# Batch 0 of an attention and GEGLU kernel in three parts of queries, with its first q and k loaded uncast

## The chip, the cores and the metric

The kernel runs on one core of a Trainium2 chip. The metric is the device time of one execution in microseconds (us), lower is better. The names of the engines in the profile are PE (TensorE), PEld (its weight loads), ACT (ScalarE), DVE (VectorE), POOL (GpSimd) and SP (the queue of SyncE). "The opening" is the time up to the first FFN block that is computed on all its 512 tokens with nothing of batch 0's attention left to do.

## The reference, cut to what matters

Sliding-window attention with a linear bias, on 8 batches, 8 heads, 576 tokens and head size 64, then an FFN on the 4608 tokens together.

```python
scores = scale * np.matmul(q, k.transpose(0, 1, 3, 2))
mask = (rel >= 0) & (rel < window)               # window = 128
scores = np.where(mask, scores + bias[None], -1000000000.0)
...                                              # softmax over the keys
x = attn_out.transpose(0, 2, 1, 3).reshape(B * S, H * D)
g = x @ w_gate                                   # 512 -> 1536
gelu = 0.5 * g * (1.0 + erf(g * inv_sqrt2))
return (gelu * (x @ w_val)) @ w_out              # 1536 -> 512
```

The kernel takes and gives float32 and computes in bf16.

## The kernel before

Everything after batch 0 is a dense stream of matmuls, with the attention of later batches laid between FFN blocks. Only batch 0 has nothing in front of it to hide behind. It is done in two parts of queries, 320 and 256. One part goes through these steps: transposes of q and k on PE and copies out of PSUM; scores on PE; exponentials on ACT; a multiplication by the mask on DVE; row sums on PE; a reciprocal on DVE; a spread of the reciprocals over partitions on PE with copies out; values on PE; a multiplication on DVE, which writes `xT`, the input of the FFN.

```python
# loads of batch 0: all on POOL, which casts float32 to bf16 on the way
load_runs(0, 0, 4)                  # q and k, heads 0 to 3, tokens 0 to 383
...
nc.gpsimd.affine_select(out=ident, ...)
load_runs(0, 4, 8)                  # heads 4 to 7
nc.gpsimd.iota(tmpl, ...)           # template of the mask
...                                 # two selects on tmpl
load_runs(1, 0, 8)                  # tokens 384 to 575
...
load_v(0)
for n in range(4):
    load_w(step * n, step * (n + 1))        # gate and value weights, by quarters
...
# the opening, in PE's program order (keep_busy(n): n matmuls of zeros before the next bank)
keep_busy(9)
first((0, 1))                       # transposes of heads 0 to 3
keep_busy(2)
scores(0, 0, (0, 1), ...)
...
spread_pe(0, 0)
values(0, 0, range(4))              # xT of 320 tokens
sums(0, 1)
for f in range(2):
    gate_val(0, f, 0, 320)          # FFN blocks 0 and 1, first 320 tokens
spread_pe(0, 1)
gate_val(0, 2, 0, 320)
values(0, 1, range(4))              # xT of the other 256 tokens
for f in range(3):
    gate_val(0, f, 320, 512)
# then blocks 3 to 11 on 512 tokens each
```

The matmuls of zeros are there to bring PE up to its full rate and to keep it there while it waits. Exponentials of the template (`emask`, eight on ACT) give the mask for all heads.

The softmax here doesn't subtract the row's maximum and nothing guards it: scores larger than these inputs give would overflow.

## Time and profile before

| | kernel before |
|---|---|
| time, median of 4 runs | 366.65 us (366.53 to 366.88) |
| span of the profiled run | 364.9 us |
| PE, DVE, ACT, POOL busy | 96%, 52%, 51%, 30% |
| first transposes of q / first scores | 5.15 / 7.58 us |
| first FFN matmul | 22.02 us |
| block 3 (first on 512 tokens) / block 6 | 30.59 / 35.77 us |

The busy shares say that PE is the bound on the whole; the times of the opening say where it isn't. Columns of the timeline: start us, length us, engine, line, operation, output<-inputs, shapes, count; in brackets the idle time before it and what ended it.

```profile
5.88 0.60 PE L70 MATMUL ps<-zeros 128*128 128x512 bf16 x2
6.57 0.36 PEld L139 LDWEIGHTS <-ks 128*64 128x64 bf16 x12 [0.58 <-DMA ks<-in_k_dram]
```

A pair of warm-up matmuls takes 0.60 us here, so PE is at its full rate by 5.88 us. The nine warm-up matmuls before that took 4.02 us, one every 0.43 us; a pair at that pace takes 1.03 us, as later traces show. This is called the half rate below. The first weights of k are loaded at 6.57 us, released by k's landing; it is the last load that the first scores need.

### The profile page before, as it was taken

The page shows a single profiled execution, that of the slowest core. Times are in us where ns is not written, and L with a number is a line of the kernel's source. Part 1 is how long each engine was busy: PE and PEld are TensorE (multiplying, and loading weights), DVE is VectorE, ACT ScalarE, POOL GpSimd, SP SyncE. Part 2 cuts the span into 40 slices and gives each one's busy share as a digit, 9 for nine tenths or more (in the row PEclk, how much of TensorE's full clock was granted, in tenths as well). Part 3 has the DMA queues.
Part 4 walks back from the last instruction along what each step waited for, and adds up shares of the span by engine and source line. Part 5 has one row for each costly group of instructions (what it writes and reads, how often), then busy time and mean ns, then how long its engine had stood idle before and what let it go on. Part 6 is the DMA issues. An engine that isn't in the chain of part 4 may idle for free.

```text
span 364.9 us, 6652 instructions
## 1 busy us (share of the span) xinstructions
PE 351.6 (96%) x2638; PEld 170.7 (47%) x2682; DVE 189.0 (52%) x307; ACT 187.2 (51%) x339; POOL 108.1 (30%) x140
## 2 busy tenths in 40 slices
PE   8889999999999999999999999999999999999995
PEld 3455545444454445444444444444444444444442
DVE  4794448533795469474547554745564404302320
ACT  5953487435966376933783278436842223323321
POOL 8945859923519203900940040000000000000000
PEclk9999999999999999999999999999999999999999
DMA  9999999999999994999991992092206030011002
GB/s 105 133 202 180 171 160 183 178 152 194 140 150 98 147 105 81 147 106 224 116 202 53 224 91 89 32 216 58 88 31 131 0 115 2 0 60 58 0 31 86
DMA packets 151168, 41.41 MB, mean 113 GB/s; under 512 B 138816, under 2 KB 144448, under 8 KB 151136
## 3 DMA queue, kind: packets, MB, share of 16 engines
q0 software_dynamic: 112608, 18.88, 67.9%
q1 hardware_dynamic: 38528, 22.10, 28.4%
q8 instruction: 21, 0.34, 0.4%
q14 instruction: 11, 0.09, 0.1%
HBM read 42.47 MB, written 9.51 MB: 142 GB/s over the span
## 4 chain that ended last, share of the span: by engine, by line
PE 86%; ACT 8%; DVE 2%; issue 1%; POOL 1%; POOLq 0%; ACTq 0%; DVEq 0%
PE ps L292 50%; PE ps L308 23%; ACT P L181 6%; PE ps L273 4%; PE ps L174 4%; PE ps L232 2%; PE ps L255 1%; DVE xT L279 1%; DVE P L184 1%; ACT L181 1%; ACT emask L359 1%; PE ps L153 1%; DVE r L241 0%; POOL ks L115 0%; ACT osb L313 0%
## 5 line engine op out<-in xcount | busy, mean ns | idle before, releaser
L297 DVE TENSOR_TENSOR hT<-ps,gelu 128x512 bf16<-128x512 f32 (+2 forms) x111 | 74.4, 674 | 121.8 <-PE ps L292 107.1
L296 ACT ACTIVATE gelu<-ps 128x512 bf16<-128x512 f32 (+2 forms) x111 | 64.9, 586 | 120.0 <-PE ps L292 119.8
L292 PE MATMUL ps<-xT,wg 128*128 128x512 bf16 (+2 forms) x430 | 111.0, 373 | 1.7 <-DVE xT L279 0.7
L292 PE MATMUL ps<-xT,wv 128*128 128x512 bf16 (+2 forms) x435 | 110.4, 373 | 0.6
L308 PE MATMUL ps<-wo,hT 128*128 128x512 bf16 x413 | 97.2, 380 | 1.5 <-issue 0.8
L181 ACT ACTIVATE P<-ps 128x512 bf16<-128x512 f32 x144 | 74.3, 629 | 6.9 <-PE ps L174 6.8
L292 PEld LDWEIGHTS <-wv 128*128 128x128 bf16 x444 | 43.3, 98 | 50.5 <-issue 0.5
L292 PEld LDWEIGHTS <-wg 128*128 128x128 bf16 x444 | 41.9, 98 | 49.8 <-issue 2.3
L184 DVE TENSOR_TENSOR P<-P,emask 128x1024 bf16<-128x1024 bf16 x72 | 48.3, 685 | 31.2 <-ACT P L181 30.9
L308 PEld LDWEIGHTS <-hT 128*128 128x128 bf16 x432 | 39.7, 98 | 49.0 <-issue 4.4
L95 POOL DMA_DIRECT2D vb<-in_v_dram x40 | 33.7, 867 | 71.1 <-PE ps L273 70.4
L313 ACT COPY osb<-ps 128x512 f32<-128x512 f32 x36 | 21.7, 602 | 37.2 <-PE ps L308 32.8
L95 POOL DMA_DIRECT2D qs<-in_q_dram x35 | 29.7, 878 | 25.5 <-DMA qT<-qs 12.9
L95 POOL DMA_DIRECT2D ks<-in_k_dram x35 | 29.6, 882 | 9.6 <-DMA qs<-in_q_dram 6.6
L241 DVE RECIPROCAL r<-ps 128x320 f32<-128x320 f32 (+1 forms) x16 | 30.7, 1938 | 2.6 <-PE ps L232 2.6
L174 PE MATMUL ps<-qT,kT 64*128 64x256 bf16 (+1 forms) x384 | 23.5, 245 | 2.2 <-ACT kT L147 0.6
L279 DVE TENSOR_TENSOR xT<-ps,rb 128x320 bf16<-128x320 f32 (+1 forms) x64 | 24.7, 448 | 0.5 <-DMA rb<-rd 0.5
L174 PEld LDWEIGHTS <-kT 64*128 64x128 bf16 x384 | 12.9, 94 | 17.2 <-issue 12.7
L273 PE MATMUL ps<-P,vb 128*64 128x128 bf16 (+2 forms) x384 | 18.4, 243 | 0.1
L273 PEld LDWEIGHTS <-vb 128*64 128x64 bf16 x384 | 14.7, 110 | 6.8 <-issue 6.8
L232 PE MATMUL ps<-P,ones 128*32 128x128 bf16 (+2 forms) x384 | 10.8, 243 | 1.3 <-DVE P L184 1.1
L232 PEld LDWEIGHTS <-ones 128*32 128x32 bf16 x384 | 7.9, 96 | 5.5 <-issue 4.7
(50 smaller groups left out, 98.7 us busy)
## 6 DMA issues: line engine op xcount, KB each, us to landing
out_dram<-osb SPq DMA_DIRECT2D x36, 256.0 KB, 2.3
rb<-rd SPq DMA_DIRECT2D x8, 576.0 KB, 7.4
vb<-in_v_dram POOLq DMA_DIRECT2D x32, 128.0 KB, 5.7
qs<-in_q_dram POOLq DMA_DIRECT2D x28, 128.0 KB, 6.9
ks<-in_k_dram POOLq DMA_DIRECT2D x28, 128.0 KB, 6.3
wg<-in_moe_w_gate_dram POOLq DMA_DIRECT2D x4, 384.0 KB, 10.7
wv<-in_moe_w_val_dram POOLq DMA_DIRECT2D x4, 384.0 KB, 11.9
wo<-in_moe_w_out_dram POOLq DMA_DIRECT2D x2, 768.0 KB, 11.3
```

The costliest lines, as they stand in the source:

```text
L95: nc.gpsimd.dma_start(out=t[lo:128, j, :].rearrange("p (h d) -> p h d", h=H), in_=src[b][:, 128 * j - 64 + lo:128 * j + 64, :].rearrange(" ...
L174: nc.tensor.matmul(out=ps[:, col:col + 128 * n].rearrange("p (n t) -> p n t", n=n), lhsT=blocks(kT, b, i, c, j, 1).rearrange("p n t -> p ( ...
L181: nc.scalar.activation(out=dst, in_=src, func=AF.Exp, scale=0.125)
L184: nc.vector.tensor_tensor(out=dst, in0=dst, in1=m, op=ALU.mult)
L232: nc.tensor.matmul(out=ps[32 * c:32 * c + 32, a:e], lhsT=ones[:, min(j, 1), i, :], rhs=prob(b, s, c, i, j, e - a), start=(i == 0 and j == ...
L241: nc.vector.reciprocal(sumrow[b][:, lo:hi], ps[:, 0:hi - lo])
L273: nc.tensor.matmul(out=ps[64 * i:64 * i + 64, a:e], lhsT=vb[b % 2][:, j, 64 * h:64 * h + 64], rhs=prob(b, s, c, i, j, e - a), start=(j == ...
L279: nc.vector.tensor_tensor(out=xT[:, c, b * S + lo:b * S + hi], in0=ps[:, 0:hi - lo], in1=recip[b][:, c, lo:hi], op=ALU.mult)
L292: nc.tensor.matmul(out=ps[:, 0:hi - lo], lhsT=w[:, c, 128 * f:128 * (f + 1)], rhs=xT[:, c, t0 + lo:t0 + hi], start=(c == 0), stop=(c == 3))
L296: nc.scalar.activation(out=gl[:, 0:hi - lo], in_=pg[:, 0:hi - lo], func=AF.Gelu)
L297: nc.vector.tensor_tensor(out=hid[g][:, f, lo:hi], in0=pv[:, 0:hi - lo], in1=gl[:, 0:hi - lo], op=ALU.mult)
L308: nc.tensor.matmul(out=po, lhsT=hid[g][:, f, 128 * t:128 * (t + 1)], rhs=wo[:, f, :], start=(f == 0), stop=(f == NF - 1))
```

## The change

Its intent: q and k of the first queries should arrive sooner, because they come on the SP and ACT queues beside POOL's own loads; a smaller first part (192 tokens) should be through attention sooner; and six FFN blocks instead of three should be begun before the last part of the attention is done (the first three of them on those 192 tokens), so that PE has useful work meanwhile. The loads on SP and ACT come uncast, so DVE casts. The core of the diff:

```diff
-PART = ((0, 320), (320, 576))
+PART = ((0, 320), (320, 576), (0, 192), (192, 320))
...
-    load_runs(0, 0, 4)
+    raw = h_pool.tile([128, NF, 512], BF16, name="hT")...bitcast(FP32)
+    load_run(0, raw[0], q, nc.sync)          # tokens 0 to 191, uncast
+    load_run(0, raw[1], k, nc.scalar)
...
+    load_run(1, runs(qs[0], 1), q, nc.gpsimd)    # tokens 192 to 575, cast by POOL
     nc.gpsimd.affine_select(out=ident, ...)
-    load_runs(0, 4, 8)
     ...                                          # template of the mask
+    load_run(1, runs(ks[0], 1), k, nc.gpsimd)
+    load_v(0, (0, 1))
+    load_w(0, step)
...
-    keep_busy(9)
-    first((0, 1))
...
+    for w in (0, 1):
+        dve(out=runs((qs, ks)[w][0], 0), in_=raw[w])
+    keep_busy(7)
+    for w in (0, 1):
+        transpose_runs(0, w, range(4), dve)
+        keep_busy(2)
+    scores_first()
...
+    scores2(0, (1, 2), lambda: (spread_pe(0, 2, (dve, dve)), values(0, 2, range(4))))
+    scores(0, 1, (0, 1), lambda: (keep_busy(3), sums(0, 3)))
...
+    gate_val(0, 0, 0, 192, tails)
+    gate_val(0, 1, 0, 192, tails)
+    values(0, 3, range(4))
...
+    for f in range(3):
+        gate_val(0, f, 192, 320)
+    gate_val(0, 3, 0, 320)
     spread_pe(0, 1)
-    gate_val(0, 2, 0, 320)
+    gate_val(0, 4, 0, 320)
     values(0, 1, range(4))
-    for f in range(3):
+    gate_val(0, 5, 0, 320)
+    for f in range(6):
         gate_val(0, f, 320, 512)
```

More of the change, by code (lines that the diff above doesn't have):

```diff
@@ L12 @@
 ENG = mybir.EngineType
-PART = ((0, 320), (320, 576))
+PART = ((0, 320), (320, 576), (0, 192), (192, 320))
 PIECES = (((0, 0, 192), (1, 64, 320), (2, 192, 320)),
-          ((2, 0, 128), (3, 0, 256), (4, 128, 256)))
-PCOL = ({0: 64, 1: 256}, {4: 0, 2: 128, 3: 256})
+          ((2, 0, 128), (3, 0, 256), (4, 128, 256)),
+          ((0, 0, 192), (1, 64, 192)),
+          ((1, 0, 128), (2, 0, 128)))
+PCOL = ({0: 64, 1: 256}, {4: 0, 2: 128, 3: 256}, {0: 0, 1: 192})
 @with_exitstack
@@ L101, in load_qk, with load_run, load_v @@
         load(ks[b % 2], k, b)
-    RUNS = ((0, 128, 3), (384, 96, 2))
+    RUNS = ((0, 96, 2), (192, 128, 3))
     def runs(t, n):
         first, parts, r = RUNS[n]
-        lo = 1536 * n
+        lo = 1024 * n
         return t.rearrange("p j x -> p (j x)")[0:parts, lo:lo + 512 * r].rearrange(
             "p (h x) -> p h x", h=H)
-    def load_runs(n, h0, h1):
+    def load_run(n, dst, src, engine):
         first, parts, r = RUNS[n]
-        for t, src in ((qs[0], q), (ks[0], k)):
-            nc.gpsimd.dma_start(
-                out=runs(t, n)[:, h0:h1, :],
-                in_=src[0][h0:h1, first:first + parts * r, :].rearrange(
-                    "h (p r) d -> p h (r d)", r=r))
-    def load_v(b):
-        load(vb[b % 2], v, b)
+        engine.dma_start(
+            out=dst,
+            in_=src[0][:, first:first + parts * r, :].rearrange("h (p r) d -> p h (r d)", r=r))
+    def load_v(b, js=range(5)):
+        load(vb[b % 2], v, b, js)
     def load_w(lo, hi):
@@ L131, in by_pair, with transpose_runs @@
         return t.rearrange("p j c t -> p (j c t)").rearrange("p (c x) -> p c x", c=4)
-    def transpose_runs(n, what, c, ps):
+    def transpose_runs(n, what, cs, copy):
         first, parts, r = RUNS[n]
         src = runs((qs, ks)[what][0], n)
-        for x in range(r):
-            for i in (0, 1):
-                nc.tensor.transpose(
-                    out=ps[64 * i:64 * i + 64, parts * x:parts * x + parts],
-                    in_=src[:, 2 * c + i, 64 * x:64 * x + 64],
-                    identity=ident[0:parts, 0:parts])
-    def untangle(copy, n, what, c, ps):
-        first, parts, r = RUNS[n]
-        dst = by_pair((qT, kT)[what][0])[:, c, 64 + first:64 + first + parts * r]
-        copy(out=dst.rearrange("p (x r) -> p x r", r=r),
-             in_=ps[:, 0:parts * r].rearrange("p (r x) -> p x r", r=r))
+        ps = bank().bitcast(BF16)
+        for k, c in enumerate(cs):
+            for x in range(r):
+                lo = parts * (r * k + x)
+                for i in (0, 1):
+                    nc.tensor.transpose(
+                        out=ps[64 * i:64 * i + 64, lo:lo + parts],
+                        in_=src[:, 2 * c + i, 64 * x:64 * x + 64],
+                        identity=ident[0:parts, 0:parts])
+        for k in range(0, len(cs), 2):
+            lo = parts * r * k
+            dst = by_pair((qT, kT)[what][0])[
+                :, cs[k]:cs[k] + 2, 64 + first:64 + first + parts * r]
+            copy(out=dst.rearrange("p c (x r) -> p c x r", r=r),
+                 in_=ps[:, lo:lo + 2 * parts * r].rearrange("p (c r x) -> p c x r", c=2, r=r))
     def transpose(b, what, c, copy):
@@ L184, in mask, with scores2, scores_first, scores @@
         nc.vector.tensor_tensor(out=dst, in0=dst, in1=m, op=ALU.mult)
-    def scores2(b):
-        P = p2_pool.tile([128, 4, 2, 128], BF16, name="P2")
-        probs2[b] = P
-        ps = [bank(), bank()]
-        for c in range(4):
-            for i in (0, 1):
-                score(b, c, i, 2, 2, 1, ps[i], 128 * c)
-        for i in (0, 1):
-            exp(P[:, :, i, :], ps[i].rearrange("p (c n) -> p c n", c=4))
-        mask(P.rearrange("p c i n -> p (c i) n"), emask[:, :, 0:128])
-    def scores(b, s, cs, then=None):
+    def scores2(b, js=(2,), then=None):
+        pss = []
+        for j in js:
+            ps = [bank(), bank()]
+            pss.append(ps)
+            for c in range(4):
+                for i in (0, 1):
+                    score(b, c, i, j, 2, 1, ps[i], 128 * c)
+        if then:
+            then()
+        for j, ps in zip(js, pss):
+            P = p2_pool.tile([128, 4, 2, 128], BF16, name="P2")
+            probs2[b, j] = P
+            for i in (0, 1):
+                exp(P[:, :, i, :], ps[i].rearrange("p (c n) -> p c n", c=4))
+            lo = 128 * (2 - j)
+            mask(P.rearrange("p c i n -> p (c i) n"), emask[:, :, lo:lo + 128])
+    def scores_first():
+        pss = []
+        for c in range(4):
+            ps = [bank(), bank()]
+            pss.append(ps)
+            for j, a, e in PIECES[2]:
+                for i in (0, 1):
+                    col = PCOL[2][j]
+                    nc.tensor.matmul(
+                        out=ps[i][:, col:col + e - a],
+                        lhsT=by_pair(kT[0])[64 * i:64 * i + 64, c, 128 * j:128 * j + 128],
+                        rhs=by_pair(qT[0])[64 * i:64 * i + 64, c, 64 + a:64 + e],
+                        start=True, stop=True)
+        for c, ps in enumerate(pss):
+            P = p_pool[0].tile([128, 2, 512], BF16, name="P")
+            probs[0, 2, c] = P
+            for i in (0, 1):
+                exp(P[:, i, 0:320], ps[i][:, 0:320])
+            mask(P[:, :, 0:192], emask[:, 2 * c:2 * c + 2, 64:256])
+            mask(P[:, :, 192:320], emask[:, 2 * c:2 * c + 2, 0:128])
+    def scores(b, s, cs, then=None, later=None):
         pss = []
@@ L215, in scores, with prob @@
                 exp(P[:, i, :], ps[i])
-            mask(P.rearrange("p i (n x) -> p i n x", n=2),
-                 emask[:, 2 * c:2 * c + 2, :].unsqueeze(2).to_broadcast((128, 2, 2, 256)))
-    def prob(b, s, c, i, j, n):
-        if (s, j) == (0, 2):
-            return probs2[b][:, c, i, 0:n]
-        return probs[b, s, c][:, i, PCOL[s][j]:PCOL[s][j] + n]
+            args = (P.rearrange("p i (n x) -> p i n x", n=2),
+                    emask[:, 2 * c:2 * c + 2, :].unsqueeze(2).to_broadcast((128, 2, 2, 256)))
+            if later is None:
+                mask(*args)
+            else:
+                later.append(args)
+    def prob(b, s, c, i, j, a, e):
+        if s == 3 or (s, j) == (0, 2):
+            return probs2[b, j][:, c, i, 0:e - a]
+        return probs[b, s, c][:, i, PCOL[s][j]:PCOL[s][j] + e - a]
     sumrow, recip = {}, {}
@@ L228, in sums @@
         ps = bank()
-        for j, a, e in PIECES[s]:
+        for n, (j, a, e) in enumerate(PIECES[s]):
             for i in (0, 1):
@@ L233, in sums @@
                         out=ps[32 * c:32 * c + 32, a:e],
-                        lhsT=ones[:, min(j, 1), i, :], rhs=prob(b, s, c, i, j, e - a),
-                        start=(i == 0 and j == 2 * s), stop=(i == 1 and j == 2 * s + 2),
+                        lhsT=ones[:, min(j, 1), i, :], rhs=prob(b, s, c, i, j, a, e),
+                        start=(i == 0 and n == 0), stop=(i == 1 and n == len(PIECES[s]) - 1),
                         skip_group_check=True)
-        if s == 0:
+        if b not in sumrow:
             sumrow[b] = r_pool.tile([128, S], FP32, name="r")
@@ L249, in spread_dma, with spread_pe @@
                 in_=d[:, i, :].unsqueeze(0).to_broadcast((64, 4, S)))
-    def spread_pe(b, s):
+    def spread_pe(b, s, copies=(nc.scalar.copy, nc.vector.tensor_copy)):
         lo, hi = PART[s]
@@ L260, in spread_pe @@
         for c, ps in enumerate(pss):
-            copy = nc.scalar.copy if c % 2 == 0 else nc.vector.tensor_copy
-            copy(out=recip[b][:, c, lo:hi], in_=ps[:, 0:hi - lo])
+            copies[c % 2](out=recip[b][:, c, lo:hi], in_=ps[:, 0:hi - lo])
     def values(b, s, cs):
@@ L269, in values @@
             pss.append(ps)
-            for j, a, e in PIECES[s]:
+            for n, (j, a, e) in enumerate(PIECES[s]):
                 for i in (0, 1):
@@ L275, in values @@
                         lhsT=vb[b % 2][:, j, 64 * h:64 * h + 64],
-                        rhs=prob(b, s, c, i, j, e - a),
-                        start=(j == 2 * s), stop=(j == 2 * s + 2), skip_group_check=True)
+                        rhs=prob(b, s, c, i, j, a, e),
+                        start=(n == 0), stop=(n == len(PIECES[s]) - 1),
+                        skip_group_check=True)
         for c, ps in zip(cs, pss):
@@ L283, with gate_val @@
     hid = {}
-    def gate_val(g, f, lo=0, hi=512):
+    def gate_val(g, f, lo=0, hi=512, later=None):
         if g not in hid:
@@ L294, in gate_val, with act @@
                     rhs=xT[:, c, t0 + lo:t0 + hi], start=(c == 0), stop=(c == 3))
-        gl = g_pool.tile([128, 512], BF16, name="gelu")
-        nc.scalar.activation(out=gl[:, 0:hi - lo], in_=pg[:, 0:hi - lo], func=AF.Gelu)
-        nc.vector.tensor_tensor(out=hid[g][:, f, lo:hi], in0=pv[:, 0:hi - lo],
-                                in1=gl[:, 0:hi - lo], op=ALU.mult)
+        def act():
+            gl = g_pool.tile([128, 512], BF16, name="gelu")
+            nc.scalar.activation(out=gl[:, 0:hi - lo], in_=pg[:, 0:hi - lo], func=AF.Gelu)
+            nc.vector.tensor_tensor(out=hid[g][:, f, lo:hi], in0=pv[:, 0:hi - lo],
+                                    in1=gl[:, 0:hi - lo], op=ALU.mult)
+        if later is None:
+            act()
+        else:
+            later.append(act)
     acc = {}
@@ L315, in out_half @@
             nc.sync.dma_start(out=out[r0:r0 + 128, :], in_=osb)
-    load_runs(0, 0, 4)
+    raw = h_pool.tile([128, NF, 512], BF16, name="hT").rearrange(
+        "p f t -> p (f t)").bitcast(FP32)
+    raw = [raw[0:96, 1024 * w:1024 * w + 1024].rearrange("p (h x) -> p h x", h=H)
+           for w in (0, 1)]
+    load_run(0, raw[0], q, nc.sync)
+    load_run(0, raw[1], k, nc.scalar)
     zeros = consts.tile([128, 512], BF16, name="zeros")
@@ L336 @@
             base=base, pattern=[[step, 128]], channel_multiplier=chan)
-    load_runs(1, 0, 8)
+    load_run(1, runs(ks[0], 1), k, nc.gpsimd)
+    load_v(0, (0, 1))
+    step = DFF // 4
+    load_w(0, step)
     for c in range(4):
@@ L341 @@
             base=-32 * c, pattern=[[-16, 2], [0, 64]], channel_multiplier=1)
-    load_v(0)
-    step = DFF // 4
-    for n in range(4):
+    load_w(step, 2 * step)
+    load_v(0, (2, 3, 4))
+    for n in (2, 3):
         load_w(step * n, step * (n + 1))
@@ L363 @@
     act, dve = nc.scalar.copy, nc.vector.tensor_copy
-    def first(cs):
-        for w in (0, 1):
-            if w and len(cs) == 2:
-                keep_busy(2)
-            for c in cs:
-                ps = bank().bitcast(BF16)
-                transpose_runs(0, w, c, ps)
-                untangle(act if c == 3 else dve, 0, w, c, ps)
-    def rest(cs, copy):
-        for c in cs:
-            for w in (0, 1):
-                ps = bank().bitcast(BF16)
-                transpose_runs(1, w, c, ps)
-                untangle(copy, 1, w, c, ps)
-    keep_busy(9)
-    first((0, 1))
-    keep_busy(2)
-    scores(0, 0, (0, 1), lambda: (keep_busy(1), first((2,))))
-    first((3,))
-    scores2(0)
-    keep_busy(2)
-    scores(0, 0, (2, 3), lambda: rest((0, 1), dve))
-    keep_busy(4)
-    scores(0, 1, (0, 1), lambda: (keep_busy(2), sums(0, 0)))
-    rest((2, 3), act)
-    keep_busy(1)
-    scores(0, 1, (2, 3))
-    keep_busy(3)
-    spread_pe(0, 0)
-    values(0, 0, range(4))
+    for w in (0, 1):
[5 more added lines that the diff above has]
+    scores_first()
+    transpose_runs(1, 0, (0, 1), act)
+    transpose_runs(1, 0, (2, 3), act)
+    keep_busy(4)
+    sums(0, 2)
+    keep_busy(2)
+    transpose_runs(1, 1, (0, 1), act)
+    transpose_runs(1, 1, (2, 3), dve)
+    keep_busy(3)
+    scores2(0, (1, 2), lambda: (spread_pe(0, 2, (dve, dve)), values(0, 2, range(4))))
+    scores(0, 1, (0, 1), lambda: (keep_busy(3), sums(0, 3)))
+    masks = []
+    scores(0, 1, (2, 3), None, masks)
+    spread_pe(0, 3, (act, act))
+    tails = []
+    gate_val(0, 0, 0, 192, tails)
+    gate_val(0, 1, 0, 192, tails)
+    values(0, 3, range(4))
+    for args in masks:
+        mask(*args)
+    gate_val(0, 2, 0, 192, tails)
+    for tail in tails[0:2]:
+        tail()
     sums(0, 1)
-    for f in range(2):
-        gate_val(0, f, 0, 320)
+    tails[2]()
+    for f in range(3):
+        gate_val(0, f, 192, 320)
+    gate_val(0, 3, 0, 320)
     spread_pe(0, 1)
-    gate_val(0, 2, 0, 320)
+    gate_val(0, 4, 0, 320)
     values(0, 1, range(4))
-    for f in range(3):
+    gate_val(0, 5, 0, 320)
+    for f in range(6):
         gate_val(0, f, 320, 512)
@@ L447 @@
             load_v(g + 2)
-        for f in range(3 if g == 0 else 0, NF):
+        for f in range(6 if g == 0 else 0, NF):
             gate_val(g, f)
```

## The prediction

> **What bounds the kernel now.** The page of the kernel before comes first: TensorE (PE) is busy for 96% of the span, the granted clock is full in all slices, and half of the chain that ended last is gate/value matmuls. So the body is a PE stream, and only a stretch where PE lacks useful work can be shortened. The table of busy time by stretch shows where that is.
>
> ```profile
> 10.00:12.00 2.00, 1.07 (x12) 0.56 (x14) 1.34 (x3) 1.68 (x5) 2.00 (x3) 1.00 1.46 107
> ...
> 20.00:22.00 2.00, 1.20 (x36) 0.76 (x31) 2.00 (x6) 1.40 (x2) 0.76 (x2) 1.00 1.31 202
> 22.00:24.00 2.00, 1.77 (x10) 0.95 (x11) 2.00 (x4) 0.44 (x1) 0.94 (x2) 1.00 1.31 203
> ```
>
> Columns after the length: busy us (and instructions) of PE, weight load, DVE, ACT, POOL, then clock, DMA share, GB/s. PE has holes early, and from 18 to 24 us DVE has none: there the vector engine sets the pace. PE busy also flatters this stretch, since 24 of its matmuls before 19 us multiply zeros only to hold the clock (8.8 us of busy time). The timeline gives the edges of the opening:
>
> ```profile
> 5.15 0.61 PEld L139 LDWEIGHTS <-qs 128*64 128x64 bf16 x12 [0.84 <-DMA qs<-in_q_dram]
> 5.79 2.56 ACT L359 ACTIVATE emask<-tmpl 128x256 bf16<-128x256 f32 x8 [3.76 <-POOL tmpl L334]
> 7.58 0.85 PE L174 MATMUL ps<-qT,kT 64*128 64x256 bf16 x8
> 8.26 2.03 ACT L181 ACTIVATE P<-ps 128x512 bf16<-128x512 f32 x4
> 11.36 5.07 ACT L181 ACTIVATE P<-ps 128x512 bf16<-128x512 f32 x10 [0.32 <-PE ps L174]
> 16.17 2.16 DVE L241 RECIPROCAL r<-ps 128x320 f32<-128x320 f32 x1 [0.74 <-PE ps L232]
> 20.14 1.28 ACT L296 ACT_TABLE_LOAD   x1
> 22.02 1.40 PE L292 MATMUL ps<-xT,wg 128*128 128x320 bf16 x4 [0.69 <-DVE xT L279]
> 22.98 1.75 DVE L241 RECIPROCAL r<-ps 128x256 f32<-128x256 f32 x1
> 29.27 0.49 PE L292 MATMUL ps<-xT,wg 128*128 128x192 bf16 x4
> 30.59 1.03 PE L292 MATMUL ps<-xT,wg 128*128 128x512 bf16 x3
> 35.77 1.03 PE L292 MATMUL ps<-xT,wg 128*128 128x512 bf16 x4
> ```
>
> Columns: start, length, engine, line, operation, shapes, count, idle time before and its releaser. First q arrives at 5.15 us, first scores at 7.58, first FFN matmul at 22.02, whole 512-token blocks from 30.59. Three whole blocks follow (8 matmuls per 1.727 us), so block 6 begins at 35.77. **That is my yardstick:** both kernels do the same from block 6 on, and PE is then nearly gapless, so the end should move by what block 6 moves.
>
> **What the skill says.** "DMA: Bandwidth & Descriptors", section "SWDGE vs HWDGE vs iDMA": casting needs the GpSimd path, and SP/ACT issues have a first-byte latency near 0.6 us against about 1 us. In this trace a POOL load of q took 3.7 to 4.4 us from issue to landing; no SP or ACT load of this kind is in it, so that gain is untested here. "VectorE: DVE Perf Modes", the perf-mode tier table: an fp32 copy within SBUF runs at two elements per cycle. The trace has no such copy. My estimate from that and its clock, 0.96 GHz: 1024/2/0.96 = 533 ns plus some 100 ns fixed, about 0.65 us each. "SBUF — State Buffer", section "Who interferes with whom": such a copy and a GpSimd operation lock each other out, so a cast may wait for a POOL descriptor write (0.76 to 0.90 us each here) or hold one up. "ScalarE: Activation LUTs", section "What ACT_TABLE_LOAD costs": 1283 ns; the trace has 1.28 us at 20.14, agreed. A second load to gelu is not added, but its place moves.
>
> **The change, part by part.**
>
> *Loads.* Two SP/ACT loads of 0.39 MB each replace four POOL issues; two casts of 0.65 us are added on DVE. Issue at 0.7 us; from rates between 160 and 200 GB/s early in the trace (written bytes, half the read bytes) I estimate landings at 3.9 and 4.4 us. Cast q ends at 4.6, transposes start about 4.65 instead of 5.15. Seven warm-up matmuls instead of nine (the nine took 4.02 us) fit that. POOL reaches the mask template two issues sooner, so the emask exponentials run near 3.7 to 6.3 instead of 5.79 to 8.35: ACT is free in time.
>
> *First part, 192 queries.* Sixteen 96-wide transposes, 0.65 us per tensor (0.04 each in the trace), then two copies of 384 columns (0.46 apart) each: q copied by 6.5, k by 7.1 and 7.6. First scores at 7.15, 0.4 us earlier than before. Eight exponentials of 320 columns: the 512-column pitch of 0.507 less 192 x 0.833 ns is 0.35 us, so 7.4 to 10.3. Last masks 10.9. Sums end 11.5. Reciprocal of 192 columns: 2.16 and 1.75 us for 320 and 256 give 6.4 ns a column, hence 1.34; done 12.95.
>
> *Remaining keys.* ACT copies of 768 columns (0.70 apart, extrapolated from 192 and 384 columns at 0.22 and 0.38) end 11.8 for q; after the sums PE transposes k, and its copies end near 13.5 (ACT) and 14.3 (DVE). The middle scores run to 14.55; the spread of the reciprocals, four DVE copies of 0.27, ends 16.1; four multiplications of 0.27 end 17.3. **The first 192 tokens of xT are ready at 17.3**, against 21.8 to 23 for 320 tokens before.
>
> *What delays their use.* PE runs in program order. The middle masks (two of 0.60 on DVE) go behind those multiplications: 18.55. Sums of part 3 end 19.0, reciprocal 19.95 (0.93 for 128 columns). The last scores follow those sums, and their exponentials end 21.3. PE can begin FFN blocks 0 and 1 at about 20.4: 8 matmuls of 192 in 0.66 us each. The ACT spread copies end 22.0, part-3 values 22.3, their multiplications 23.1; then the deferred masks to 24.35 and sums of part 1 to 25.1. Two hidden multiplications come first on DVE, then the 256-column reciprocal: 26.95, against 24.73 before.
>
> *Payback.* By then six pieces of 192 and 128 tokens of blocks 0 to 2 are done or waiting for a PSUM bank: eight banks, with block 2's pair held until its product on DVE after the reciprocal. I count up to 0.85 us of such waiting, and PE continuous from about 27.3. What remains: block 3 on 320 tokens 1.09, spread 0.70, block 4 1.09, values 1.0, block 5 1.09, six pieces of 192 at 0.66 = 3.96, and 0.1 waiting: 9.0 us. Block 6 starts at 36.3. Were the bank wait absent it would be 35.45. Against 35.77 the sum is thus +0.5 to -0.3 us. The reason for so little: earlier FFN work (about 3 us moved ahead of the last reciprocal) is paid for by the last part of attention being ready some 2.2 us later, and by three times as many reciprocal, spread and value rounds in a DVE stretch that is already full.
>
> **Rivals.** (a) *The early FFN fills real holes and little is given back*: PE has 0.9 and 0.8 us idle in the two worst slices shown and the warm-up matmuls hide several more. The author's tuned counts of warm-up matmuls suggest attention to these holes. If masks, bank releases and copies are each 0.2 us better than my chain, block 6 starts around 34 and the time is about 364.8. (b) *DVE becomes the bound*: it gets 1.3 us of casts, four 0.27 spread copies all on DVE and an extra reciprocal; the reciprocals' fixed part alone (2.16 - 320 x 6.4 ns = 0.11) is small, but ordering puts the long one behind other work. Then block 6 slips to 37 or 38 and the time to 368. (c) *The new loads contend*: uncast q and k double the written bytes, all queues work on the same DMA data paths, and the casts lock against POOL. If q lands at 5 us instead of 3.9 the whole chain slips by 1 us: about 367.5. (d) *Weights or values arrive late*: weights now issue from about 6 us instead of 12.92, and the last three v tiles go behind them. Estimated from 0.2 MB/us for weights and 0.12 for v, v tile 2 lands near 19 and is wanted near 22, so it should hide. Even a gain at this end is limited later: the next batch's k last issues at 35.86 and needs 5 us, close to its use at 41.2; but the weights' earlier issue should move that too.
>
> **Range and chances.** My chain gives -0.3 to +0.5 us; I lean toward rival (a) by another 0.4 because a schedule this carefully interleaved probably fills some waits I counted in full. That puts the time at 366.54 - 0.3 = 366.2 us. The landing time of the loads is uncertain by 1 us, the DVE and bank chain by about 1.5 us, so 364.0 to 368.3 should hold it 8 times in 10. Faster by over 2% needs 7.3 us, block 6 at 28.4: before the last reciprocal plus six partial blocks could be done even in the best case. Slower by over 2% needs block 6 at 43, which only a serious load stall could make. So 2% faster, 96% the same, 2% slower.
>
> **What will show it.** First transposes near 4.65 (right) or at 5.2 and later (rival c). Each cast near 0.65 us; 1.1 would mean one element per cycle. First scores near 7.15, xT of 192 tokens complete near 17.3, first FFN matmul near 20.4, the 256-column reciprocal ending near 27, whole blocks from 36.3 or earlier. If DVE is busy without a gap from 15 to 28 us, (b) holds; if PE waits in front of the gate/value matmuls name DMA, (d) does. The span beyond block 6 should be equal within 0.5 us: if it isn't, the yardstick is wrong, and the later loads or clock deserve a look.

## The result and the profile after

The changed kernel takes 368.61 us (median of 4 runs, 367.91 to 368.67), before 366.65 us. The ratio of the two is 1.0048, with a 95% interval of 1.0031 to 1.0066. Here and below a ratio is the mean time of one kernel's fast runs over that of the other's fast runs of the same rounds, so it is not quite the ratio of the medians. The change is slower by half a per cent: within the 2% band, but above the predicted range, which ended at 368.3.

The timeline of the changed kernel, same columns as before:

```profile
1.20 3.17 PE L73 MATMUL ps<-zeros 128*128 128x512 bf16 x7 [1.20 <-DVE zeros L370]
...
5.74 0.83 DVE L418 CAST qs<-hT 96x1024 bf16<-96x1024 f32 x1 [2.46 <-DMA hT<-in_q_dram]
6.04 0.85 POOL L126 DMA_DIRECT2D wg<-in_moe_w_gate_dram  x1
6.50 0.87 DVE L418 CAST ks<-hT 96x1024 bf16<-96x1024 f32 x1
6.63 0.66 PEld L143 LDWEIGHTS <-qs 96*64 96x64 bf16 x16 [3.17 <-DVE qs L418]
...
7.41 1.03 PE L73 MATMUL ps<-zeros 128*128 128x512 bf16 x2
...
8.37 0.66 PEld L143 LDWEIGHTS <-ks 96*64 96x64 bf16 x16 [0.84 <-DVE qT L151]
...
9.16 1.03 PE L73 MATMUL ps<-zeros 128*128 128x512 bf16 x2
...
10.12 1.25 PE L218 MATMUL ps<-qT,kT 64*128 64x192 bf16 x16
...
18.73 1.14 DVE L316 TENSOR_TENSOR xT<-ps,rb 128x192 bf16<-128x192 f32 x4
...
23.01 0.51 PE L329 MATMUL ps<-xT,wg 128*128 128x192 bf16 x4
...
27.63 1.76 DVE L278 RECIPROCAL r<-ps 128x256 f32<-128x256 f32 x1 [0.16 <-PE ps L269]
...
37.95 1.03 PE L329 MATMUL ps<-xT,wg 128*128 128x512 bf16 x3
```

Line by line: the seven warm-up matmuls end at 4.37 us, but q is cast only from 5.74 us, so PE stands still for 2.3 us. When it goes on, a pair of warm-up matmuls takes 1.03 us instead of the 0.60 of before: PE is at half its rate. It has not fallen to it: the seven warm-up matmuls, 3.17 us for seven, ran at the half rate too, and PE had not come up yet. The first scores run at 10.12 us, 2.5 us later than before. Block 6 begins at 37.95 us against 35.77, 2.18 us later. From there on the changed kernel needs 366.8 - 37.95 = 328.85 us and the kernel before 364.9 - 35.77 = 329.13 us. So all of the loss comes from the opening. The 0.28 us is no more than the spread of this stretch: in the other profiles below, e2 apart, it is 328.8 to 329.0 us.

The chain of waits of the changed kernel (start us, length us, what) says the same from the other end:

```profile
0.75 4.97 DMA hT<-in_q_dram
...
5.74 0.84 DVE qs L418
6.59 0.04 issue
6.63 0.85 PE ps L143 x16
7.48 0.96 PE ps L73 x2
```

The path to the last instruction starts with the load of q, goes through its cast and then through warm-up matmuls. Work that was put in to fill idle time is on the path.

### The profile page after: what moved, and what is told of

Read it like the earlier page. It is cut to its first block, busy times and chain, and to the rows that moved or that the text cites. A ratio compares the mean times of both kernels' runs of the same rounds, so it can differ in the third digit from the quotient of the medians.

```text
span 366.8 us, 6848 instructions
## 1 busy us (share of the span) xinstructions
PE 352.1 (96%) x2715; PEld 175.3 (48%) x2759; DVE 191.3 (52%) x322; ACT 188.3 (51%) x346; POOL 105.3 (29%) x136
## 3 DMA queue, kind: packets, MB, share of 16 engines
HBM read 42.47 MB, written 9.51 MB: 142 GB/s over the span
## 4 chain that ended last, share of the span: by engine, by line
PE 88%; ACT 5%; DVE 3%; DMA 1%; issue 1%; ACTq 0%
PE ps L329 50%; PE ps L352 23%; PE ps L309 4%; ACT P L185 4%; PE ps L178 4%; PE ps L269 2%; PE ps L292 1%; DMA hT<-in_q_dram 1%; DVE P L188 1%; PE ps L73 1%; PE ps L143 1%; DVE xT L316 1%; DVE r L278 1%; ACT L185 1%; PE ps L157 1%
## 5 line engine op out<-in xcount | busy, mean ns | idle before, releaser
L336 DVE TENSOR_TENSOR hT<-ps,gelu 128x512 bf16<-128x512 f32 (+3 forms) x117 | 75.0, 647 | 119.2 <-PE ps L329 105.5
L335 ACT ACTIVATE gelu<-ps 128x512 bf16<-128x512 f32 (+3 forms) x117 | 65.6, 564 | 117.4 <-PE ps L329 116.2
L329 PE MATMUL ps<-xT,wv 128*128 128x512 bf16 (+3 forms) x459 | 111.5, 362 | 0.6
L329 PE MATMUL ps<-xT,wg 128*128 128x512 bf16 (+3 forms) x454 | 111.0, 362 | 0.7
L185 ACT ACTIVATE P<-ps 128x512 bf16<-128x512 f32 (+1 forms) x146 | 74.0, 621 | 12.5 <-PE ps L178 8.0
L329 PEld LDWEIGHTS <-wv 128*128 128x128 bf16 x468 | 45.0, 98 | 48.6
L188 DVE TENSOR_TENSOR P<-P,emask 128x1024 bf16<-128x1024 bf16 (+1 forms) x77 | 48.7, 647 | 31.5 <-ACT P L185 30.9
L278 DVE RECIPROCAL r<-ps 128x256 f32<-128x256 f32 (+3 forms) x17 | 30.8, 1833 | 2.8 <-PE ps L269 2.8
L316 DVE TENSOR_TENSOR xT<-ps,rb 128x256 bf16<-128x256 f32 (+3 forms) x68 | 25.0, 431 | 1.9 <-PE ps L309 1.3
L178 PE MATMUL ps<-qT,kT 64*128 64x128 bf16 (+1 forms) x376 | 21.7, 243 | 0.9 <-DVE kT L160 0.4
```

The lines of the kernel that those rows point to most:

```text
L178: nc.tensor.matmul(out=ps[:, col:col + 128 * n].rearrange("p (n t) -> p n t", n=n), lhsT=blocks(kT, b, i, c, j, 1).rearrange("p n t -> p ( ...
L185: nc.scalar.activation(out=dst, in_=src, func=AF.Exp, scale=0.125)
L188: nc.vector.tensor_tensor(out=dst, in0=dst, in1=m, op=ALU.mult)
L278: nc.vector.reciprocal(sumrow[b][:, lo:hi], ps[:, 0:hi - lo])
L316: nc.vector.tensor_tensor(out=xT[:, c, b * S + lo:b * S + hi], in0=ps[:, 0:hi - lo], in1=recip[b][:, c, lo:hi], op=ALU.mult)
L329: nc.tensor.matmul(out=ps[:, 0:hi - lo], lhsT=w[:, c, 128 * f:128 * (f + 1)], rhs=xT[:, c, t0 + lo:t0 + hi], start=(c == 0), stop=(c == 3))
```

## The experiments

Two theories are tested first. Theory A: the late uncast load, its casts and the idle PE cost the time, and the three-part schedule itself is about neutral. Theory B: the three-part schedule costs the time, by its order of work on DVE. Every kernel was timed beside the kernel before on the same chip; "ratio" is to that. All results matched the reference within the comparison's tolerance.

| run | what it is | ratio, 95% interval | first scores | block 6 |
|---|---|---|---|---|
| before | | 1 | 7.58 | 35.77 |
| after | the change | 1.0048 (1.0031 to 1.0066) | 10.12 | 37.95 |
| e1 | three parts, POOL casts q and k | 1.0001 (0.9989 to 1.0012) | 8.47 | 36.73 |
| e2 | after, 15 warm-up matmuls | 1.0029 (1.0007 to 1.0050) | 9.30 | 36.99 |
| e3 | after, nothing waits for the loads | 0.9964 (0.9951 to 0.9977) | 7.40 | 35.09 |
| e4 | two parts, uncast loads | 1.0039 (1.0026 to 1.0052) | 9.86 | 38.05 |
| e5 | after, loads in halves, 11 warm-ups | 0.9995 (0.9984 to 1.0007) | 8.70 | 36.39 |
| e6 | after, both loads on one queue | one look, 367.67 us | 9.19 | 37.02 |
| e8 | three parts, q by POOL, k uncast | 1.0006 (0.9989 to 1.0023) | 9.40 | 37.11 |
| e9 | two parts, k uncast, mask earlier | 1.0012 (0.9995 to 1.0030) | 9.51 | 37.70 |
| e10 | two parts, mask earlier | 0.9999 (0.9987 to 1.0012) | 7.50 | 35.98 |
| e11 | e5 with 9 warm-ups | 0.9993 (0.9980 to 1.0005) | 8.38 | 36.06 |
| e12 | e9 with 11 warm-ups | 1.0001 (0.9988 to 1.0015) | 8.18 | 36.14 |
| e13 | e8 with 11 warm-ups | 0.9999 (0.9986 to 1.0011) | 8.30 | 35.99 |

Times in the last two columns are of the profiled execution, in us. For the two-part kernels block 6 is the start of block 3 plus 5.18 us, the distance between them in the kernel before.

### e1: the loads undone, the schedule kept

```diff
-    load_run(0, raw[0], q, nc.sync)
-    load_run(0, raw[1], k, nc.scalar)
+    load_run(0, runs(qs[0], 0), q, nc.gpsimd)
+    load_run(0, runs(ks[0], 0), k, nc.gpsimd)
-    for w in (0, 1):
-        dve(out=runs((qs, ks)[w][0], 0), in_=raw[w])
-    keep_busy(7)
+    keep_busy(9)
```

> The changed kernel with one part undone: the first q and k of 192 tokens come cast by POOL, as in the kernel before, without the casts on DVE, and nine warm-up matmuls instead of seven. Theory A (the late uncast load plus the two casts cost the time, the three-part schedule itself is worth about nothing or a little): q transposes near 5.5 us instead of 6.63, k transposes near 6.7 instead of 8.38, first scores near 8.0 instead of 10.12, block 6 near 35.7 instead of 37.95, time near 366.4, equal to before. Theory B (the three-part schedule is what costs, by DVE order): first scores earlier, but block 6 stays within 0.7 us of 37.95 and the time stays at 368.

The median was 367.05 us beside 367.04 us: the whole loss is gone, with the three-part schedule in place. From its timeline:

```profile
5.33 0.53 PE L143 MATMUL ps<-ident,qs 96*64 96x96 bf16 x16 [0.57 <-DMA qs<-in_q_dram]
...
7.29 0.53 PE L143 MATMUL ps<-ident,ks 96*64 96x96 bf16 x16 [0.89 <-DMA ks<-in_k_dram]
...
23.27 0.58 PE L309 MATMUL ps<-P,vb 128*64 128x128 bf16 x14 [0.25 <-DMA vb<-in_v_dram]
```

q is usable at 5.33 us, 1.3 us earlier than in the change, k at 7.29, later than the 6.7 that I expected. So the first scores (8.47) and block 6 (36.73) were later than my 8.0 and 35.7 too; the profiled execution, 367.51 us, was also the slowest of the five. The third line shows a new wait: values of part 3 stand in front of a v tile that was issued behind more POOL work. Theory A holds, theory B is out as the main cause.

### e2: no pause of PE

```diff
-    keep_busy(7)
+    keep_busy(15)
```

> The changed kernel with 15 warm-up matmuls instead of 7, so that PE has no pause between 4.37 us and the first transposes. Theory A with a second cause (the pause left PE at half rate: pairs of warm-up matmuls took 1.03 us instead of 0.60 and stood in front of the k transposes and the scores): q transposes stay at 6.6, k transposes near 7.75 instead of 8.38, first scores near 9.3 instead of 10.12, time 367.6 to 368.0. Rival (the half rate is hidden beside DVE and ACT): first scores move less than 0.3 us and the time stays at 368.6.

From its timeline:

```profile
7.11 0.53 PE L143 MATMUL ps<-ident,qs 96*64 96x96 bf16 x16
7.57 0.60 PE L73 MATMUL ps<-zeros 128*128 128x512 bf16 x2
...
9.30 0.91 PE L218 MATMUL ps<-qT,kT 64*128 64x192 bf16 x16
```

The pair is back at 0.60 us. From the first transposes to the first scores it is 9.30 - 7.11 = 2.19 us, against 10.12 - 6.63 = 3.49 in the change: 1.30 us of half rate were on the path. (The expected 9.3 us came true partly by luck: the transposes were later than I had said and the steps after them shorter.) Fifteen was some too many, since the transposes waited for warm-up work until 7.11, so the gain at the scores is 0.8 us. Three executions took 367.16 to 367.18 us and three 367.9 to 369.5. The profiled one was the slowest, and in it PE also waited 1.8 us for the transposing load of a later batch, a wait that no other profile here has; the mean is worse for it.

### e3: nothing waits for the loads

```diff
-        dve(out=runs((qs, ks)[w][0], 0), in_=raw[w])
+        dve(out=runs((qs, ks)[w][0], 0),
+            in_=zeros.bitcast(FP32)[0:96, 0:128].unsqueeze(1).to_broadcast((96, H, 128)))
```

> The changed kernel, but the two casts read a zeroed tile instead of the loaded one, so nothing waits for the SP and ACT loads (which still run). Wrong result on purpose. Theory A: casts begin near 3.35 instead of 5.74, q transposes near 4.4, first scores near 7.2, block 6 near 35.5, time near 366.2: without the wait, the change would just break even with before. Theory B: the time stays above 367.5 although the first scores come 2.5 us earlier.

The loads still run, but the first 192 tokens of batch 0 use zeros. (The comparison passed even so: with inputs of size 0.1 these scores are near 0.01, so zeros change the softmax little.) From its timeline:

```profile
3.05 1.77 POOL L384 TENSOR_SCALAR_AFFINE_SELECT tmpl<-tmpl 128x128 f32<-128x128 f32 x2
3.21 0.62 DVE L418 CAST qs<-zeros 96x1024 bf16<-96x1024 f32 x1
3.75 0.67 DVE L418 CAST ks<-zeros 96x1024 bf16<-96x1024 f32 x1
...
4.30 0.85 PE L143 MATMUL ps<-ident,qs 96*64 96x96 bf16 x16
5.08 1.03 PE L73 MATMUL ps<-zeros 128*128 128x512 bf16 x2
...
7.40 0.92 PE L218 MATMUL ps<-qT,kT 64*128 64x192 bf16 x16
...
24.77 1.76 DVE L278 RECIPROCAL r<-ps 128x256 f32<-128x256 f32 x1 [0.16 <-PE ps L269]
```

With the wait gone the three-part schedule is 0.36% faster than before, and block 6 starts at 35.09 us. From the last reciprocal to block 6 it is 10.32 us here and 10.32 in the change (37.95 - 27.63): what follows the load is the same in both, only shifted. The first three lines show the shared port between DVE and POOL. Casts that met no descriptor writes took 0.62 and 0.67 us; two selects on POOL that took 0.54 us in the change took 1.77 beside them. The line at 5.08 us matters for the reading of e2: here PE went from its warm-up matmuls to the transposes without a pause, and was at half rate all the same; the next pair, at 6.67 us, took 0.60. So a pause isn't needed for the half rate. Seven warm-up matmuls were too few to bring PE up by 5.08 us, and in the change it was still not up at 10.12.

### e4: the uncast loads alone, in the old schedule

```diff
-    load_runs(0, 0, 4)
+    for eng, h0 in ((nc.sync, 0), (nc.scalar, 4)):
+        for w, src in enumerate((q, k)):
+            eng.dma_start(out=raw[w][:, h0:h0 + 4, :], in_=src[0][h0:h0 + 4, 0:384, :]...)
...
+    casts(0)                   # heads 0 to 3; those of heads 4 to 7 after first((0, 1))
     keep_busy(9)
     first((0, 1))
```

> The kernel before with one part of the change done alone: the first q and k (384 tokens here) come uncast by the SP and ACT queues and are cast on DVE, the two-part schedule is kept. Theory A: q lands near 5 us or later and is cast after that, so the first scores come 1.5 to 3 us later than 7.58 and the time is 368 to 369.5. Theory B: the loads cost little by themselves, the time stays within 0.7 us of 366.6.

The loads alone, without the schedule, cost 0.39%: nearly the whole loss of the change. (They are larger here, 384 tokens, and in halves of four heads; and after a pause of 1.38 us PE made its transposes of k at half rate, from 8.11 us. So the 0.39% holds the wait and the half rate together.) Two casts of the same size from its timeline, each with what POOL did at that time:

```profile
4.33 1.79 POOL L345 TENSOR_SCALAR_AFFINE_SELECT sel<-sel 128x128 f32<-128x128 f32 x4
5.05 0.56 DVE L388 CAST qs<-hT 128x768 bf16<-128x768 f32 x1 [1.77 <-DMA hT<-in_q_dram]
...
6.07 4.24 POOL L95 DMA_DIRECT2D vb<-in_v_dram  x5
7.18 0.87 DVE L388 CAST ks<-hT 128x768 bf16<-128x768 f32 x1 [1.57 <-DMA hT<-in_k_dram]
```

Beside a row of POOL loads the cast took 0.87 us, beside the selects 0.56. It isn't always the cast that is held up: in e11 the cast of q took 0.69 us beside a POOL load, and two POOL loads of v took 1.92 us there instead of the 1.57 of the change.

### e5, e6 and e11: why the uncast q lands late

In the trace of the change, packets of the two hardware queues in two half microseconds, 2.5 to 3.0 and 3.5 to 4.0 us (queue and kind: packets, MB, share of 16 engines; q1 is SP's queue with q, q10 is ACT's with k):

```profile
q1 hardware_dynamic: 158, 0.08, 70.0%
q10 hardware_dynamic: 14, 0.01, 4.7%
```

```profile
q10 hardware_dynamic: 171, 0.09, 57.7%
q1 hardware_dynamic: 170, 0.09, 57.4%
```

q's load was issued at 0.75 us and its first packets moved at 1.87 us. Almost alone, its queue moved 158 packets in half a microsecond, with the engines at 70%. With both queues active it was 341 together, and q got half. By 2.5 us it had moved only 144 of its packets. q has 768 packets of 512 bytes, so it could not be through before 4.5 us; the last ones moved between 4.5 and 5.0 us, and another 0.7 to 1.2 us passed until DVE could start. Two edits test this. e5 lets both queues carry q first (heads 0 to 3 on one, 4 to 7 on the other) and then k; e6 puts both loads on SP, k behind q.

```diff
 # e5
-    load_run(0, raw[0], q, nc.sync)
-    load_run(0, raw[1], k, nc.scalar)
+    for w, src in enumerate((q, k)):
+        for h0, eng in ((0, nc.sync), (4, nc.scalar)):
+            eng.dma_start(out=raw[w][:, h0:h0 + 4, :], in_=src[0][h0:h0 + 4, 0:192, :]...)
-    keep_busy(7)
+    keep_busy(11)
 # e6
-    load_run(0, raw[1], k, nc.scalar)
+    load_run(0, raw[1], k, nc.sync)
```

> The changed kernel with its two uncast loads cut in halves of four heads: both queues carry q first and k after it; eleven warm-up matmuls. Theory A1 (one such queue alone moves about 300 packets in a us, and q competes with k for the rest, so q lands late): q lands near 4.7 us instead of 5.7, transposes near 5.6, first scores near 8.2 instead of 10.12, block 6 near 36, time 366.6. Theory A2 (a fixed delay of the queues sets the landing): q still lands after 5.4 and the time stays above 367.3.

> The changed kernel with k's load behind q's on the same SP queue, so that k can't compete with q. A1, if k's traffic is what delays q: q lands near 4.5 us and k after 7. Rival (one queue's own rate of about 300 packets in a us delays q): q lands near 5.2 to 5.4 (768 packets in 2.5 us from 1.87, and about 1 us from last packet to landing), k after 7.5, and the time is 0.5 to 1.5 us longer than that of the change.

The first cast, from the timelines of e5 and then e6:

```profile
4.35 0.69 DVE L420 CAST qs<-hT 96x1024 bf16<-96x1024 f32 x1 [1.06 <-DMA hT<-in_q_dram]
```

```profile
5.13 0.69 DVE L418 CAST qs<-hT 96x1024 bf16<-96x1024 f32 x1 [1.84 <-DMA hT<-in_q_dram]
```

q was usable at 4.35 us with both queues on it, at 5.13 with one queue and no k beside it, and at 5.74 in the change. The same loads differ by up to 0.23 us between two profiles (5.74 and 5.59 in e2, 4.35 and 4.58 in e11), less than either step. So k's load on the other queue cost about 0.6 us, and having q on one queue, in one piece, instead of on two, in halves, about another 0.8; pieces and queues are not separated. No fixed delay of the queues explains this. Nor does the pace that both expectations gave as one queue's own, about 300 packets in a microsecond. In e6 SP's queue had all packets to itself, and moved these from 2.5 to 3.0 and from 3.0 to 3.5 us:

```profile
q1 hardware_dynamic: 245, 0.13, 89.0%
```

```profile
q1 hardware_dynamic: 344, 0.17, 114.7%
```

One queue alone thus reached what two reached together in the change. By 3.5 us it had moved 727 packets, so q's 768 were nearly through (if they go in the order of the queue), but q was usable only at 5.13. That e6 came close to the landing that the rival named (5.2 to 5.4) was luck. What the runs leave of the single queue's cost is a slower start (383 packets by 3.0 us in e6, 509 on both queues in e5) and a longer way from the last packets to the cast; why is open. My expectation for e6's time was wrong: its one look took 367.67 us, less than the change, because k on one queue was cast from 6.56 us, hardly later than the 6.50 of the change, and because PE came up earlier in this execution: after the same seven warm-up matmuls and a pause of 1.50 us it made q's transposes and the next pair of warm-up matmuls (0.60 us) at the full rate. The pair after k's transposes, at 8.22 us, took 1.03 again.

In e5 q was cast by 5.04 us, but eleven warm-up matmuls at half rate held PE until 6.01. e11 therefore has nine.

> The halves experiment with nine warm-up matmuls instead of eleven: there q was cast by 5.04 us but PE still had warm-up work until 5.97, at half rate. If PE's readiness is what is left of the load wait: q transposes near 5.1, k transposes near 6.8, first scores near 8.0 instead of 8.7, block 6 near 35.7, time 0.2 to 0.3 per cent under before. If PE stays at half rate: block 6 near 36.2 and the time equals before.

q was transposed at 5.32 us, but the cast of k ended at 6.93 and k was transposed at 6.99, so the scores came at 8.38, not at 8.0. The ratio of 0.9993 has an interval that includes 1. The change with its loads in halves is thus as fast as the kernel before, not shown faster.

### e8 and e13, e9 and e12, e10: can a mixture beat both?

e8 lets POOL cast q while SP and ACT bring k in halves. e9 takes the two-part kernel and gives it k of the first heads uncast and an earlier mask. e10 has the earlier mask alone.

```diff
 # e8, from the change
-    load_run(0, raw[0], q, nc.sync)
-    load_run(0, raw[1], k, nc.scalar)
+    load_run(0, runs(qs[0], 0), q, nc.gpsimd)
+    for h0, eng in ((0, nc.sync), (4, nc.scalar)):
+        eng.dma_start(out=raw[1][:, h0:h0 + 4, :], in_=k[0][h0:h0 + 4, 0:192, :]...)
 ...                               # one cast, keep_busy(9), v tile 2 with tiles 0 and 1
 # e9, from the kernel before
-    load_runs(0, 0, 4)
+    for h0, eng in ((0, nc.sync), (2, nc.scalar)):
+        eng.dma_start(out=raw[:, h0:h0 + 2, :], in_=k[0][h0:h0 + 2, 0:384, :]...)
+    load_run0(qs, q, 0, 4)
+    load_run0(qs, q, 4, 8)
 ...                               # template of the mask, then load_run0(ks, k, 4, 8); one cast
 # e10, from the kernel before: the template's four instructions move ahead of
     load_runs(0, 4, 8)
```

> The changed kernel with q of the first 192 tokens cast by POOL, k uncast in halves by SP and ACT, one cast on DVE, the third v tile issued earlier, nine warm-up matmuls. If the load wait was the cost and the rest of my chain holds: q transposes near 5.3 us, k cast done near 5.6, first scores near 7.4, block 6 near 35.1, time 0.2 per cent under before. If contention of POOL with the two queues delays q: q transposes after 6 and the time equals before or more.

> The two-part kernel before with two ideas of the change: k of the first four heads comes uncast on SP and ACT (two heads each, one cast on DVE), and the mask template is made before k of the last four heads is issued. In the kernel before, ACT's mask exponentials (5.79 to 8.35) and the landing of k at 6.57 held the first exponential back to 8.35. If ACT's chain is what bounds that opening: first scores near 6.9, first exponential near 7.2, whole blocks from 29.6 instead of 30.59, time 0.3 per cent under before. If DVE bounds it: first exponential earlier but whole blocks stay within 0.3 us of 30.59.

> The two-part kernel before with only the mask template made before q and k of the last four heads are issued on POOL. If ACT's chain bounds the opening: first exponential near 7.9 instead of 8.26, whole blocks from 30.2 instead of 30.59, time 0.1 per cent under before. If the later q and k (issued 0.9 us later) bind instead: whole blocks at 30.6 to 31.2, time equal or 0.1 per cent over.

None was faster. In e8 and e9 q, cast by POOL, came at 5.9 and 6.0 us, beside the uncast k, instead of 5.33 (e1) and 5.15 (before): the expected contention. In e10 the first exponential ran at 7.92 us instead of 8.26, but k of the last heads, issued later, stopped PE for 0.68 us at 9.83, and block 3 began at 30.80 us instead of 30.59: the gain was handed to the next load.

Both e8 and e9 had two groups of times: three executions at 366.3 to 366.5 us and three at 367.8 to 368.05 for e8; two at 368.4 and four at 366.6 to 366.9 for e9. Both profiles fell into the slow group, so no quick execution of the two can be looked at. From e9's timeline:

```profile
6.01 0.85 PE L139 MATMUL ps<-ident,qs 128*64 128x128 bf16 x12 [0.78 <-DMA qs<-in_q_dram]
...
6.79 1.03 PE L70 MATMUL ps<-zeros 128*128 128x512 bf16 x2
```

After a pause of 0.78 us PE was at half rate, as it had been in all of its nine warm-up matmuls (4.02 us for nine; in e10 nine took 3.44, because the last of them ran at full rate). e12 and e13 are e9 and e8 with `keep_busy(11)` for `keep_busy(9)`.

> The two-part kernel with k of the first heads uncast and the mask earlier, now with eleven warm-up matmuls instead of nine. With nine, three executions took 366.6 to 366.9 us and two 368.4; the profiled one of 368.46 had PE at half rate after a pause of 0.8 us. If that pause is the cause: all executions near 366.3, none near 368.4, whole blocks near 30.3. If it isn't: the two groups of times stay.

> The three-part kernel with q cast by POOL and k uncast in halves, now with eleven warm-up matmuls instead of nine, so that PE has no pause before q at 5.9 us. With nine, three executions took 366.3 to 366.5 us and three 367.8 to 368.05. If the half rate of PE is the cause: all executions near 366.2, first scores near 8.1 instead of 9.4. If it isn't: two groups stay.

From e12's timeline:

```profile
6.17 0.53 PE L139 MATMUL ps<-ident,qs 128*64 128x128 bf16 x12 [0.87 <-DMA qs<-in_q_dram]
6.63 0.60 PE L70 MATMUL ps<-zeros 128*128 128x512 bf16 x2
```

Here the pause was even longer, 0.87 us, and PE kept its full rate, because it had already reached it: the eleven warm-up matmuls, 4.09 us for eleven, passed from half to full rate at about 4.4 us. The slow groups are gone (366.42 to 367.56 and 366.59 to 367.05 us, five executions of each, on another chip than e8 and e9). So the length of the pause alone doesn't decide, but also whether PE had come up to its full rate before it; e4's pause of 1.38 us shows that it can be lost again. My 366.3 and 366.2 us were not reached, and e12's whole blocks began at 30.96, not 30.3: the groups went as expected, the gain didn't come. With q at 6.1 us both kernels end level with before, so nothing here beats both.

## Why the prediction was wrong

Part of the mechanism was told as rival (c), with its size missed; the cost of a single queue for q and PE's half rate were in no part of the prediction. Point by point:

- **The step that failed** is in the part on loads: "from rates between 160 and 200 GB/s early in the trace (written bytes, half the read bytes) I estimate landings at 3.9 and 4.4 us". q was usable at 5.74 us, and k was cast from 6.50. The rates were taken from POOL's casting queue at a time when it was already flowing. The new queues start slowly (first packet 1.1 us after issue, 144 of 768 packets by 2.5 us), k's load takes its part of the packets once it runs (171 beside q's 170 in half a microsecond), and q is usable only 0.7 us or more after its last packet. e6 and e5 show that k's load beside it and the single queue each cost time; where in the start and the end the single queue loses it stays open.
- **The supporting inference failed too**: "Seven warm-up matmuls instead of nine ... fit that". I read the new count as a sign of an early landing. It was a count that left PE idle for 2.3 us.
- **A term was absent from the sum**: PE's half rate. From transposes to scores I had 2.50 us; the change took 3.49, and e2, with PE at its full rate, 2.19. I had read "the granted clock is full in all slices"; but that column also says 1.00 for 1 to 5 and 6.6 to 10 us of the change, where PE's matmuls came at half rate, so it doesn't show this. In every profile the first warm-up matmuls ran at half rate, and PE came up at a moment that differs: nine of them took 3.44 us in e10, where the last ones were already faster; before, a pair took 0.60 at 5.88 us; in e3, without a pause, a pair still took 1.03 at 5.08; in e5, without a pause, one still took 0.79 at 6.79. The Trainium skill, "TensorE: Matmul & The Clock Gate", Part 1, says that the full clock comes after a free-running window of about 3.4 us of activity, so that the moment of the switch varies between runs. That fits what is seen here. That the window is the reason is taken from the page; the runs show the half rate, its cost and its cure (more warm-up matmuls). What the pause of 2.26 us added in the change is not settled: the one of 1.50 us in e6 did no harm, and e3 had none.
- **The cast** took 0.83 us instead of 0.65. The lock between DVE and POOL that the prediction named is there: 0.62 and 0.67 us in e3, 0.56 against 0.87 for equal casts in e4, and POOL's selects stretched from 0.54 to 1.77 us. In e11 it was POOL's loads that took longer, and the cast 0.69.
- **The rest of the chain was right, and a little pessimistic.** From first scores to block 6 I had 36.3 - 7.15 = 29.15 us, of which 0.85 was waiting for PSUM banks. It took 27.83 us; PE had no such wait, as the list of its waits has none before gate/value matmuls. Against my 36.3 the sum is: load 5.74 - 3.95 = +1.79, cast to transposes +0.19, transposes to scores +0.99, scores to block 6 -1.32; together +1.65, which is 37.95.
- **The yardstick held**: from block 6 on the two kernels differ by 0.28 us, within the 0.5 that I had allowed, and the three-part kernel e3, whose transposes began at 4.30 where I had 4.65, reached block 6 at 35.09 where I had 35.45 without bank waits.
- **Rival (a)**, that early FFN work fills holes, is true but small: from first scores to block 6 the kernel before needs 28.19 us, the three-part one 27.83. In these two profiles its whole worth is 0.4 us, less than the load lost. **Rival (b)**, DVE as the new bound, is refuted by e1 and e3. **Rival (d)**, late v tiles, did not show in the change but did in e1, at 0.25 us. The lean of 0.4 us on how carefully the schedule was made had no ground in the profile.

What stays open: why e2 waited 1.8 us for a later batch's transposing load in its profile, why one queue brings q so much later than two although it can move as many packets, and what sets the moment at which PE comes up in an execution.

## What to carry to other kernels

A load moved to another queue has another start, another pace and another company; a landing time should be measured on that queue before a schedule is built on it, and where several loads are needed in order, let all queues carry the first one first. Filler work has to bring PE to its full rate before the data is there: too little of it cost 1.3 us here, how much is enough differs between executions, and where it stands between real steps at half rate it joins the critical path. Look at the time of a known matmul, not at the column of the granted clock, to see which rate it has. To judge a change in an opening, find the instant after which both kernels do the same, and follow both to it.

## What the Trainium skill lacked or had wrong

- "DMA: Bandwidth & Descriptors", "Latency and other measured facts", gives a first-byte latency near 0.6 us for SP and ACT issues. Here SP's first packet of q moved 1.1 us after the start of its issue (0.75 to 1.87 us), of which the issuing instruction itself took 0.39; ACT's first packets of k, issued at the same time, moved only between 2.5 and 3.0 us. That second delay is in no page.
- The same page says that issuing from several engines only saves issue time. The packets agree: one queue alone moved 344 packets of 512 bytes in half a microsecond (e6), two together 341 (the change). The landing doesn't: q divided over both queues was usable at 4.35 us (e5), on one queue, with nothing on the other, at 5.13 (e6).
- "TensorE: Matmul & The Clock Gate", Part 1, puts the step to the full rate at around 4 us of sustained matmuls, give or take 0.5 us. The first matmul was at 1.20 us in each run here. In e10 nine warm-up matmuls took 3.44 us, so that the last ones ran at full rate before 4.64 us; in e5 a pair at 6.79 us, more than 5.5 us after the first, was still slow (0.79 us), after matmuls without a pause.
- "SBUF — State Buffer" was right about the lock: casts of 768 columns took 0.56 us and, beside POOL's loads, 0.87 (e4); casts of 1024 columns took 0.62 and 0.67 (e3) and up to 1.00 (k in e6). It gives 1.5 as one measured factor for a GpSimd instruction that is held up; here two selects of 0.54 us took 1.77.
